# Batch 2's q turned by DMA, and the loads of k gathered behind the copies of v

## The chip, the cores and the metric

One NeuronCore of a Trainium2 chip runs the whole program. The metric is device time in microseconds (us) for one launch. Five engines work side by side, each through its own list in order: PE (matrix products), DVE and ACT (element-wise work), POOL (here also the issuer of all loads from HBM) and SP (here the issuer of DMA transposes and of the stores). They wait for each other by semaphores.

## The reference

Sliding-window attention feeds a two-layer network. For 8 batches, 8 heads, 576 positions and a head size of 64:

```python
scores = (q @ k.transpose(0, 1, 3, 2)) / sqrt(64)
mask = (rel >= 0) & (rel < 64)          # rel = query position - key position
attn = softmax(where(mask, scores, -1e9))
x = (attn @ v).transpose(0, 2, 1, 3).reshape(4608, 512)
h = x @ w_in                            # 512 -> 2048
out = (h * cos(h)) @ w_out              # 2048 -> 512, float32
```

## The kernel before

The 4608 rows of x are cut into 9 tiles of 512 rows, and the network runs tile by tile. Tile 0 and the attention of batches 0 and 1 run in a first part whose order is written out in a long string. After it comes a loop over the tiles 1 to 8; one pass is called a stage here, and stage n is the pass over tile n. In the span of the profiled execution stage 1 starts at 57.4 us, stage 2 at 90.0, stage 3 at 120.5, stage 4 at 150.9, stage 5 at 181.6 and stage 6 at 212.0.

In a stage PE multiplies x by `w_in` (L500, 64 products of 512 columns into `h_ps`); ACT takes the sine (L730) and DVE multiplies it with h (L733); then PE multiplies the result by `w_out` (L744, 64 more products). The last two tiles do this second product by a Strassen-like scheme with 7 products (L587). Between these products PE is given the attention of one batch: stage n scores batch n+1.

The order of that attention work is a plan of due times. A stage has 32 slots; `at(time, fn, ...)` puts a step into the plan, and `pump(time)`, called after every four or so products, emits all steps that are due. What is emitted goes to the end of its engine's list, so a slot sets only the order on each engine; when a step runs is decided by what stands ahead of it and by its semaphores. These steps matter here:

- `load_chunk` (L183) loads 128 rows of q or k of one batch, all heads, cast to bf16, issued on POOL. A batch has 5 chunks, the last one of 64 rows. `load_v` (L189) does the same for v.
- `spread_v` (L127 by the helper `copy`) copies half of v's rows on POOL, so that every window of 128 keys is contiguous.
- `turn_q` and `turn_k` (L244) are DMA transposes issued on SP. Three of them turn the 5 chunks (0 and 1, 2 and 3, 4) of q into `qT` and of k into `kT`. For batch 2, q is instead transposed by PE (`tr_q`, L227, five transposes for each of four head pairs) and copied out of PSUM by DVE (`put_q`, L127).
- `burst_scores` (L331) emits the scores of a batch in two bursts, at slots 14.6 and 20.2. Burst one scores blocks 0 to 3 of the sequence, so it reads chunks 0 and 1 of `qT` and `kT`: the first of the three transposes of each. Burst two reads the others.
- Each group of four score blocks then goes through `g_max` (DVE, L368), `g_exp` (ACT, L380), `g_inv` (DVE, L390), `g_norm` (POOL, L397, which makes `w`) and `g_trans` (a DMA transpose on SP, L416, which makes `wT`). A batch has nine groups; from stage 3 on the first four are normalised before `spread_v` and the last five behind it (stage 1 has three behind it, stage 2 four).
- `values` (PE, L432) multiplies `wT` with v at the end of a stage, and `store` (SP, L509) writes a tile's result in two transfers of 512 KB early in the next stage.

Before the change the chunks of k and q of a batch come alternately, in three pieces: for batches 5 to 7 chunk 0 of both comes two stages ahead, behind the copies of v; chunks 1 and 2 of both and 3 and 4 of q come early in the stage that follows, and chunks 3 and 4 of k behind that stage's copies of v. The three transposes of k are due at slot 26 of that same stage, so on SP they stand ahead of the late `wT` transposes and of the stores.

Of the kernel before, what the change touches and what calls it, by code (L numbers as in the profile page):

```python
# [30 lines left out]
PAIRS = 4  # L31
Q = 16
T = 2 * Q
# [5 lines left out]
BUSY = 8  # L39
NB = 5  # L40
TURNS = ((0, 2), (2, 4), (4, 5))
TURNED = (3, 4, 5, 6, 7)
FAST = (7, 8)
PRODUCTS = ("P1", "P2", "P6", "P5", "P7", "P3", "P4")

# [26 lines left out]
def kernel(  # L72
# [9 lines left out]
    nc = tc.nc  # L82
    B, H, S, D = q.shape
# [17 lines left out]
    qsets = [const.tile([128, NB * PAIRS * 128], BF16, name=f"qT{i}") for i in range(2)]  # L101
# [5 lines left out]
    ident = const.tile([128, 128], BF16, name="ident")  # L107
# [6 lines left out]
    st = {}  # L114
# [11 lines left out]
    def copy(engine, out, in_):  # L126
        {"a": nc.scalar.copy, "p": nc.gpsimd.tensor_copy}.get(engine, nc.vector.tensor_copy)(out, in_)  # L127
# [29 lines left out]
    def head_rows(name, b, p):  # L157
        if (name, b) not in st:
            st[name, b] = rows_tile(name)
        lo = 2 * NC * D * p if b else RC * D + 2 * NC * D * (p - 1)  # L160
        return st[name, b][0:NP, lo:lo + 2 * NC * D].rearrange("p (h x) -> p h x", h=2)
# [48 lines left out]
    def transposed(name, b, p):  # L210
        t_ps = ps_t.tile([128, S], BF16, tag="t", name=f"t{name}_ps")
        of = st[name, b]
        if b == p == 0:
            for c in range(RC):
                for h in range(2):
                    d = slice(64 * h, 64 * h + 64)
                    nc.tensor.transpose(t_ps[d, 64 * c:64 * c + 64], of[d, 64 * c:64 * c + 64], ident[d, d])
        elif b < 2:
            rows = head_rows(name, b, p)
            for c in range(NC):  # L220
                for h in range(2):
                    nc.tensor.transpose(t_ps[64 * h:64 * h + 64, NP * c:NP * c + NP], rows[:, h, D * c:D * c + D],  # L222
                                        ident[:NP, :NP])
        else:
            for c in range(NB):
                n = min(128, S - 128 * c)
                nc.tensor.transpose(t_ps[:, 128 * c:128 * c + n], of[0:n, c, 128 * p:128 * p + 128], ident[0:n, 0:n])  # L227
        return t_ps


    def in_order(t_ps, to, b, p):
        c = RC if b == p == 0 else NC
        return t_ps.rearrange("d (c p) -> d p c", c=c), to.rearrange("d (p c) -> d p c", c=c)

    def by_pair(x):
        return x[:, 0:PAIRS * S].rearrange("d (h s) -> d h s", h=PAIRS)

    def by_chunk(x):
        return x.rearrange("d (c h p) -> d c h p", c=NB, h=PAIRS)
# [12 lines left out]
    def tr_q(b, p):  # L252
        st["tq", b, p] = transposed("q", b, p)

    def put_q(b, p, engine=None):
        if b > 1:
            t_ps, to = st.pop(("tq", b, p)), by_chunk(qsets[b % 2])[:, :, p]
            copy(engine, to[:, 0:4], t_ps[:, 0:512].rearrange("d (c p) -> d c p", c=4))
            copy(engine, to[:, 4, 0:64], t_ps[:, 512:S])
            return  # L260
        of, to = in_order(st.pop(("tq", b, p)), by_pair(qsets[b])[:, p], b, p)
        if b:
            copy(engine, to, of)
        elif engine == "a":
            nc.scalar.mul(to, of, scale)
        else:
            nc.vector.tensor_scalar(to, of, scale, None, ALU.mult)
# [4 lines left out]
    def tr_k(b, p):  # L272
        st["tk", b, p] = transposed("k", b, p)
# [327 lines left out]
    def at(time, fn, *args):  # L601
        plan.append((time, len(plan), fn, args))
# [8 lines left out]
    for i, (b, jobs, banks) in enumerate(bursts):  # L611
        t = T * (b - 1)
        at(t + BURST[i % 2] + 0.9 * (i == 1), burst_scores, i)
        for n in range(jobs[0][0], jobs[-1][-1] + 1):
            place = (n - n_listed) % NU
            time = t + BURST[0] + PACE * place
# [11 lines left out]

    for b in range(2, B):
        t0 = T * (b - 1)  # L630
        for lo, hi in TURNS if b in TURNED else ():
            at(t0 - T + (24.3 if b == 4 else 23.4) + 0.01 * lo, turn_q, b, lo, hi)
        for p in range(0 if b in TURNED else PAIRS):
            t_q = t0 + (2 if b == 2 else 1) + (3.3 if b == 2 else 3.5) * p
            at(t_q, tr_q, b, p)
            at(t_q + 0.02, put_q, b, p)
        if b > 2:
            for c in range(NB):
                for i, name in enumerate(("q", "k")):
                    time = 17.9 + 2.8 * i if b == 3 and c == NB - 1 else 5.6 + 1.6 * c + 0.8 * i  # L640
                    if b > 3 and name == "k" and c > 2:
                        time = (24.2 if b == 4 else 22.4) + 0.01 * c
                    if b > 4 and c == 0:
                        time = (24.26 if b == 5 else 22.46) + 0.01 * i - T
                    at(t0 - T + time, load_chunk, name, b, c)
        for lo, hi in TURNS:
            at(t0 + 0.1 * lo - (2 if b == 2 else 6), turn_k, b, lo, hi)
        for c in range(5):
            at(t0 + (8 if b == B - 1 else 0.5) + c, load_v, b, c)
        for half_ in range(2):  # L650
            if b == 2:
                at(t0 + 24.1 + 0.01 * half_, spread_v, b, half_, "p", 0, 2)
                at(t0 + 24.2 + 0.1 * half_, spread_v, b, half_, "p", 2, 4)
            else:
                at(t0 + (24 if b == 3 else 22.2) + 0.1 * half_, spread_v, b, half_)
    for mt in range(2, n_mt):
        for p in range(PAIRS):
            time = T * mt - (8.01 if mt == n_mt - 1 else 1.01)
# [8 lines left out]
    for n in range(16):  # L667
        i, f = divmod(n, 4)
# [14 lines left out]
    def spread_first(lo, hi):  # L683
# [9 lines left out]
             "io": put_steps, "mk": put_masks, "mc": cast_masks,  # L693
             "tq": lambda p: tr_q(0, p), "tk": lambda p: tr_k(0, p), "Tq": lambda p: tr_q(1, p), "Tk": lambda p: tr_k(1, p),
             "pq": lambda p, engine: put_q(0, p, engine), "pk": lambda p, engine: put_k(0, p, engine),
             "Pq": lambda p, engine: put_q(1, p, engine), "Pk": lambda p, engine: put_k(1, p, engine),
             "zA": spread_first(0, 1), "zB": spread_first(1, 3), "zC": lambda engine: spread_v(0, 1, engine, 3, 4),
             "yA": lambda engine: spread_v(1, 0, engine, 0, 2), "yB": lambda engine: spread_v(1, 0, engine, 2, 3),
# [85 lines left out]
```

## Time and profile before

| what | value |
|---|---|
| three runs, median | 301.48 us (301.41 to 301.97) |
| profiled execution, own time | 301.49 us |
| its span (first to last instruction) | 299.7 us |
| PE busy | 291.8 us, 97% of the span |
| DVE, ACT, POOL busy | 230.9, 232.3, 205.2 us |
| PE's share of the chain that ended last | 89% |

The profiled execution's own time is 1.8 us above its span. Rows of the timeline and of the chain give a start and a duration in us, then engine, line, operation, what is written and read, and how many instructions are merged. A row marked SPq or POOL with DMA in its name is the issue of a transfer, not the transfer; the time from issue to landing stands in a row of its own. "Idle before" and "<-" give how long the engine stood idle ahead of the row and what released it.

### The profile page before, as it was taken

What the parts mean: (1) busy time and instruction counts of PE and PEld (TensorE: products, weight loads), DVE (VectorE), ACT (ScalarE), POOL (GpSimd) and SP (SyncE); (2) the same over time, 40 slices, a digit from 0 to 9 for tenths busy, and PEclk for the clock granted to TensorE, in tenths of its full rate; (3) what the DMA queues carried; (4) which work ended last, traced back from release to release, by engine and by line L of the source; (5) the groups of instructions that cost most, each with busy time, mean ns of one, the idle gap of its engine ahead of it and who ended that gap; (6) DMA issues with size and microseconds to landing.
All of it is one profiled execution on the core that took longest, in us unless ns stands there. A gap on an engine that the chain in (4) does not pass through costs nothing.

```text
span 299.7 us, 8184 instructions
## 1 busy us (share of the span) xinstructions
PE 291.8 (97%) x2787; PEld 159.7 (53%) x2787; DVE 230.9 (77%) x904; ACT 232.3 (77%) x781; POOL 205.2 (68%) x226
## 2 busy tenths in 40 slices
PE   8978999999999999999999999999999999999995
PEld 3667854544454444444454545444544454784584
DVE  4998788988887786788677866887588658976793
ACT  5997699876988799869986998699969996305600
POOL 9898668993699849995999599949997850000000
PEclk9999999999999999999999999999999999999999
DMA  7999999999999995999999999999999443003013
GB/s 147 175 204 191 196 190 141 113 138 148 234 165 121 202 175 99 167 143 229 152 171 139 178 164 199 142 230 165 152 121 189 70 88 142 0 3 140 3 35 107
DMA packets 165867, 43.22 MB, mean 144 GB/s; under 512 B 153216, under 2 KB 161472, under 8 KB 165824
## 3 DMA queue, kind: packets, MB, share of 16 engines
q0 software_dynamic: 100896, 18.06, 81.6%
q1 hardware_dynamic: 64784, 24.56, 45.7%
q8 instruction: 22, 0.36, 0.5%
q14 instruction: 21, 0.17, 0.2%
q10 hardware_dynamic: 144, 0.07, 0.1%
HBM read 36.70 MB, written 9.44 MB: 154 GB/s over the span
## 4 chain that ended last, share of the span: by engine, by line
PE 89%; DMA 6%; POOL 2%; DVE 0%; issue 0%; POOLq 0%
PE h_ps L500 37%; PE out_ps L744 28%; PE out_ps L587 8%; PE out_ps L483 5%; DMA w_in<-in_moe_w_in_dram 4%; PE h_ps L464 4%; PE o_ps L432 3%; PE s_ps L331 3%; DMA q<-in_q_dram 2%; POOL v L189 1%; PE s_ps L353 1%; PE tq_ps L227 0%; POOL w_in L205 0%; PE tw_ps L413 0%; POOL q L166 0%
## 5 line engine op out<-in xcount | busy, mean ns | idle before, releaser
L500 PE MATMUL h_ps<-xT,w_in 128*128 128x512 bf16 x512 | 112.5, 379 | 0.2
L733 DVE TENSOR_TENSOR gT<-h_ps,sin 128x512 bf16<-128x512 f32 x128 | 84.9, 688 | 27.3 <-ACT sin L730 27.3
L730 ACT ACTIVATE sin<-h_ps 128x512 f32<-128x512 f32 x128 | 73.8, 598 | 34.8 <-PE h_ps L500 32.6
L380 ACT ACTIVATE e<-s,negm 128x128 f32<-128x128 f32 (+1 forms) x256 | 97.2, 382 | 1.7 <-POOL v L127 0.9
L397 POOL TENSOR_TENSOR w<-e,rden 128x512 bf16<-128x512 f32 (+1 forms) x68 | 69.0, 1029 | 28.8 <-DVE rden L390 21.1
L744 PE MATMUL out_ps<-w_out,gT 128*128 128x512 bf16 x384 | 85.3, 379 | 0.0
L500 PEld LDWEIGHTS <-w_in 128*128 128x128 bf16 x512 | 49.7, 98 | 58.3
L744 PEld LDWEIGHTS <-gT 128*128 128x128 bf16 x384 | 36.5, 98 | 43.1
L368 DVE CUSTOM_DVE_ANT_0 s<-s_ps,mask 128x128 f32<-128x128 f32 (+1 forms) x256 | 56.0, 276 | 1.8 <-PE s_ps L353 1.5
L380 ACT ACTIVATION_READ_ACCUMULATOR e<-s,negm 128x1 f32 x256 | 48.3, 189 | 0.0
L189 POOL DMA_DIRECT2D v<-in_v_dram x40 | 34.1, 877 | 0.6 <-DMA q<-in_q_dram 0.6
L183 POOL DMA_DIRECT2D q<-in_q_dram x30 | 26.4, 883 | 4.6 <-PE tq_ps L222 2.6
L183 POOL DMA_DIRECT2D k<-in_k_dram x30 | 26.3, 886 | 0.6 <-DMA v<-in_v_dram 0.6
L390 DVE RECIPROCAL rden<-den 128x4 f32<-128x4 f32 (+1 forms) x73 | 12.2, 167 | 18.4 <-ACT e L380 18.1
L127 POOL COPY v<-v 64x1536 bf16<-64x1536 bf16 (+3 forms) x16 | 22.9, 1431 | 0.4
L368 DVE DVE_READ_ACCUMULATOR2_ANT negm<- 128x1 f32 x256 | 21.0, 82 | 0.1
L127 DVE CAST xT<-o_ps 128x512 bf16<-128x512 f32 x24 | 15.5, 677 | 4.7 <-PE o_ps L432 4.5
L464 PE MATMUL h_ps<-xT,w_in 128*128 128x256 bf16 x128 | 14.6, 273 | 0.9 <-DMA w_in<-in_moe_w_in_dram 0.9
L483 PE MATMUL out_ps<-w_out,gT 128*128 128x512 bf16 x64 | 14.8, 380 | 0.0
L464 PEld LDWEIGHTS <-w_in 128*128 128x128 bf16 x128 | 12.3, 98 | 2.3 <-DMA w_in<-in_moe_w_in_dram 1.0
L587 PEld LDWEIGHTS <-sums 128*128 128x128 bf16 x136 | 12.2, 98 | 2.0 <-DVE sums L532 0.4
L470 ACT ACTIVATE sin<-h_ps 128x512 f32<-128x512 f32 x16 | 9.2, 596 | 4.3 <-PE h_ps L464 4.3
(92 smaller groups left out, 293.0 us busy)
## 6 DMA issues: line engine op xcount, KB each, us to landing
out_dram<-out_sb SPq DMA_DIRECT2D x16, 512.0 KB, 8.0
v<-in_v_dram POOLq DMA_DIRECT2D x32, 128.0 KB, 6.2
q<-in_q_dram POOLq DMA_DIRECT2D x24, 128.0 KB, 9.5
k<-in_k_dram POOLq DMA_DIRECT2D x24, 128.0 KB, 9.4
w_in<-in_moe_w_in_dram POOLq DMA_DIRECT2D x4, 512.0 KB, 8.7
w_out<-in_moe_w_out_dram POOLq DMA_DIRECT2D x4, 512.0 KB, 10.9
q<-in_q_dram POOLq DMA_DIRECT2D x7, 144.0 KB, 6.2
k<-in_k_dram POOLq DMA_DIRECT2D x7, 144.0 KB, 6.3
```

What stands on the lines that cost most here:

```text
L127: {"a": nc.scalar.copy, "p": nc.gpsimd.tensor_copy}.get(engine, nc.vector.tensor_copy)(out, in_)
L183: nc.gpsimd.dma_start(out=st[name, b][0:n, c].rearrange("p (h d) -> p h d", h=H), in_=src.rearrange("h p d -> p h d"))
L189: nc.gpsimd.dma_start(out=vt.rearrange("p (h d) -> p h d", h=H), in_=v[b, :, c * 128:c * 128 + n, :].rearrange("h p d -> p h d"))
L368: nc.vector.tensor_tensor_reduce(out=s[:, u, c], in0=s_ps[:, u, c], in1=mask[:, 2 - j % 2 if j else 0, c], scale=-scale if b else -1.0, sc ...
L380: nc.scalar.activation(e[:, u, c], s[:, u, c], AF.Exp, bias=negm[:, u:u + 1], scale=1.0 if n < n_first else -1.0, accum_out=den[:, u:u + 1])
L397: (nc.gpsimd if engine == "p" else nc.vector).tensor_tensor(out=w[:, 0:u], in0=e[:, 0:u], op=ALU.mult, in1=rden[:, 0:u].unsqueeze(2).to_br ...
L464: nc.tensor.matmul(out=h_ps[:, half * e:half * e + half], lhsT=w_in_sb[:, ks, ff * 128:ff * 128 + 128], rhs=st["xT", 0][:, ks, half * g:ha ...
L500: nc.tensor.matmul(out=st["h", ff], lhsT=w_in_sb[:, ks, ff * 128:ff * 128 + 128], rhs=st["xT", mt][:, ks], start=start, stop=stop)
L587: nc.tensor.matmul(out=to[n_] if split else to[:, e], lhsT=lhs[name][f // 2][:, f % 2, 128 * e:128 * e + 128], rhs=rhs[name][:, f, lo:hi], ...
L730: nc.scalar.activation(sin, h_ps, AF.Sin, bias=math.pi / 2.0)
L733: nc.vector.tensor_tensor(out=gt[:, e], in0=h_ps, in1=sin, op=ALU.mult)
L744: nc.tensor.matmul(out=o_ps[e], lhsT=gT[ff // 2][:, ff % 2, ms * 128:ms * 128 + 128], rhs=w_out_sb[:, ff], start=ff == 0, stop=ff == n_ff - 1)
```

## The change

Three things are done, all in the plan:

1. q of batch 2 is turned by three DMA transposes like the later batches, alternating on SP with the three of k. The 20 PE transposes and 8 DVE copies for it go, and so does the code for them.
2. All five chunks of k of batches 3 to 7 are loaded in one stretch, behind the copies of v of the stage before the one that scores them (due at slot 24.3, from batch 5 on 22.5). Their three transposes move from slot 26 of that stage to slots 1.6, 3.6 and 5.6 of the next, the stage that scores them.
3. The five chunks of q of batches 3 to 7 are loaded in one stretch, at slots 4.9 to 8.1; v's loads come 0.8 slots apart from batch 3 on, and those of batch 7 at slot 0.5 in place of 8.

The core of the diff:

```diff
-        for lo, hi in TURNS if b in TURNED else ():
-            at(t0 - T + (24.3 if b == 4 else 23.4) + 0.01 * lo, turn_q, b, lo, hi)
-        for p in range(0 if b in TURNED else PAIRS):
-            t_q = t0 + (2 if b == 2 else 1) + (3.3 if b == 2 else 3.5) * p
-            at(t_q, tr_q, b, p)
-            at(t_q + 0.02, put_q, b, p)
-        if b > 2:
-            for c in range(NB):
-                for i, name in enumerate(("q", "k")):
-                    time = 17.9 + 2.8 * i if b == 3 and c == NB - 1 else 5.6 + 1.6 * c + 0.8 * i
...
-                    at(t0 - T + time, load_chunk, name, b, c)
         for lo, hi in TURNS:
-            at(t0 + 0.1 * lo - (2 if b == 2 else 6), turn_k, b, lo, hi)
-        for c in range(5):
-            at(t0 + (8 if b == B - 1 else 0.5) + c, load_v, b, c)
+            at(t0 - (2.01 - 0.1 * lo if b == 2 else T - (24.3 if b == 4 else 23.4) - 0.01 * lo), turn_q, b, lo, hi)
+        for lo, hi in TURNS:
+            at(t0 + (0.1 * lo - 2 if b == 2 else 1.6 + lo), turn_k, b, lo, hi)
+        for c in range(NB):
+            if b > 2:
+                at(t0 - T + 4.9 + 0.8 * c, load_chunk, "q", b, c)
+                at(t0 - (7.7 if b < 5 else 9.5) + 0.01 * c, load_chunk, "k", b, c)
+            at(t0 + 0.5 + (1 if b == 2 else 0.8) * c, load_v, b, c)
```

POOL's list from the first norms of stage 3 (batch 4) to the loads early in stage 4; `v_77` is the buffer of v of batch 4, `v_78` that of batch 5, and the k loaded here is that of batch 5 (before: chunks 3 and 4 of batch 5, then chunk 0 of q and k of batch 6). Before:

```order
L397 TENSOR_TENSOR w<-e,rden 128x512 x4
L127 COPY v_77<-v_77 64x3x512
L127 COPY v_77<-v_77 64x4x512
L183 DMA k<-in_k_dram 128x8x64
L183 DMA k<-in_k_dram 64x8x64
L183 DMA q<-in_q_dram 128x8x64
L183 DMA k<-in_k_dram 128x8x64
L397 TENSOR_TENSOR w<-e,rden 128x512 x5
L189 DMA v_78<-in_v_dram 128x8x64 x4
L189 DMA v_78<-in_v_dram 64x8x64
```

After:

```order
L387 TENSOR_TENSOR w<-e,rden 128x512 x4
L126 COPY v_77<-v_77 64x3x512
L126 COPY v_77<-v_77 64x4x512
L182 DMA k<-in_k_dram 128x8x64 x4
L182 DMA k<-in_k_dram 64x8x64
L387 TENSOR_TENSOR w<-e,rden 128x512 x5
L188 DMA v_78<-in_v_dram 128x8x64 x4
L188 DMA v_78<-in_v_dram 64x8x64
L182 DMA q<-in_q_dram 128x8x64 x4
L182 DMA q<-in_q_dram 64x8x64
```

Five loads stand between the copies and the last five norms in place of four, and the loads of k early in the stage are gone.

SP's list from the first `wT` of stage 3 to the first `wT` of stage 4; `qT_76` and the `kT` here belong to batch 5, which stage 4 scores. Before:

```order
L416 DMA_TRANSPOSE wT<-w 128x4x128 x4
L244 DMA_TRANSPOSE qT_76<-q 128x8x128 x2
L244 DMA_TRANSPOSE qT_76<-q 128x4x64
L416 DMA_TRANSPOSE wT<-w 128x4x128 x2
L244 DMA_TRANSPOSE kT<-k 128x8x128 x2
L244 DMA_TRANSPOSE kT<-k 128x4x64
L416 DMA_TRANSPOSE wT<-w 128x4x128 x3
L509 DMA out_dram<-out_sb 128x2x512 x2
```

After:

```order
L406 DMA_TRANSPOSE wT<-w 128x4x128 x4
L239 DMA_TRANSPOSE qT_76<-q 128x8x128 x2
L239 DMA_TRANSPOSE qT_76<-q 128x4x64
L406 DMA_TRANSPOSE wT<-w 128x4x128 x5
L499 DMA out_dram<-out_sb 128x2x512 x2
L239 DMA_TRANSPOSE kT<-k 128x8x128 x2
L239 DMA_TRANSPOSE kT<-k 128x4x64
```

The three transposes of k have moved from between the late `wT` to behind all five of them and behind both stores.

SP's list in stage 1, from the three of k of batch 2 on. Before:

```order
L244 DMA_TRANSPOSE kT<-k 128x8x128 x2
L244 DMA_TRANSPOSE kT<-k 128x4x64
L416 DMA_TRANSPOSE wT<-w 128x4x128 x2
L509 DMA out_dram<-out_sb 128x2x512 x2
L416 DMA_TRANSPOSE wT<-w 128x4x128 x4
```

After:

```order
L239 DMA_TRANSPOSE qT_75<-q 128x8x128
L239 DMA_TRANSPOSE kT<-k 128x8x128
L239 DMA_TRANSPOSE qT_75<-q 128x8x128
L239 DMA_TRANSPOSE kT<-k 128x8x128
L239 DMA_TRANSPOSE qT_75<-q 128x4x64
L239 DMA_TRANSPOSE kT<-k 128x4x64
L406 DMA_TRANSPOSE wT<-w 128x4x128 x2
L499 DMA out_dram<-out_sb 128x2x512 x2
```

The second transpose of k has one more ahead of it, the third two more. On PE, nothing changes but that the 20 transposes and their weight loads are gone.

More of the change, by code (lines that the diff above doesn't have):

```diff
@@ L41 @@
 TURNS = ((0, 2), (2, 4), (4, 5))
-TURNED = (3, 4, 5, 6, 7)
 FAST = (7, 8)
@@ L217, in transposed @@
                     nc.tensor.transpose(t_ps[d, 64 * c:64 * c + 64], of[d, 64 * c:64 * c + 64], ident[d, d])
-        elif b < 2:
+        else:
             rows = head_rows(name, b, p)
@@ L223, in transposed @@
                                         ident[:NP, :NP])
-        else:
-            for c in range(NB):
-                n = min(128, S - 128 * c)
-                nc.tensor.transpose(t_ps[:, 128 * c:128 * c + n], of[0:n, c, 128 * p:128 * p + 128], ident[0:n, 0:n])
         return t_ps
@@ L255, in put_q @@
     def put_q(b, p, engine=None):
[L256 to L260, printed above, removed]
         of, to = in_order(st.pop(("tq", b, p)), by_pair(qsets[b])[:, p], b, p)
@@ L630 @@
         t0 = T * (b - 1)
-        for lo, hi in TURNS if b in TURNED else ():
-            at(t0 - T + (24.3 if b == 4 else 23.4) + 0.01 * lo, turn_q, b, lo, hi)
-        for p in range(0 if b in TURNED else PAIRS):
-            t_q = t0 + (2 if b == 2 else 1) + (3.3 if b == 2 else 3.5) * p
-            at(t_q, tr_q, b, p)
-            at(t_q + 0.02, put_q, b, p)
-        if b > 2:
-            for c in range(NB):
-                for i, name in enumerate(("q", "k")):
-                    time = 17.9 + 2.8 * i if b == 3 and c == NB - 1 else 5.6 + 1.6 * c + 0.8 * i
[L641 to L644, printed above, removed]
-                    at(t0 - T + time, load_chunk, name, b, c)
-        for lo, hi in TURNS:
-            at(t0 + 0.1 * lo - (2 if b == 2 else 6), turn_k, b, lo, hi)
-        for c in range(5):
-            at(t0 + (8 if b == B - 1 else 0.5) + c, load_v, b, c)
+        for lo, hi in TURNS:
+            at(t0 - (2.01 - 0.1 * lo if b == 2 else T - (24.3 if b == 4 else 23.4) - 0.01 * lo), turn_q, b, lo, hi)
[6 more added lines that the diff above has]
+            at(t0 + 0.5 + (1 if b == 2 else 0.8) * c, load_v, b, c)
         for half_ in range(2):
```

## The prediction

> **What bounds the kernel now.** I read the chain that ended last first. The rows below are from it: the four groups of PE transposes of q of batch 2 (L227), and the first burst of scores of stages 1 to 6 (L331). A row is start, duration, what. Behind it stands one row of the windows view: length of stage 3, then busy time of PE, PEld, DVE, ACT and POOL, the granted clock, the DMA share and GB/s.
>
> ```profile
> 59.98 0.35 PE tq_ps L227 x5
> 63.90 0.36 PE tq_ps L227 x5
> 66.95 0.35 PE tq_ps L227 x5
> 70.00 0.36 PE tq_ps L227 x5
> 73.05 0.52 PE s_ps L331 x32
> ...
> 103.97 0.52 PE s_ps L331 x32
> ...
> 134.44 0.52 PE s_ps L331 x32
> ...
> 164.91 0.52 PE s_ps L331 x32
> ...
> 195.55 0.52 PE s_ps L331 x32
> ...
> 226.02 0.52 PE s_ps L331 x32
> ```
>
> ```profile
> 120.44:150.90 30.46, 30.43 (x264) 14.58 (x265) 23.03 (x108) 27.07 (x95) 26.70 (x29) 1.00 1.78 177
> ```
>
> PE is busy for 30.43 of a stage's 30.46 us, at full clock, and the first bursts follow each other by 30.5 to 30.9 us. So from stage 1 on PE alone sets the pace: what leaves its list there is gained whole, and any wait that is put into it is paid whole. Nothing else has to be sped up; it must only not come late. The question is whether the data of each first burst are still early.
>
> The second view is the timeline of POOL at the end of stage 3, with the same place (norm, copies of v) of other stages. It shows when the loads of k can be issued.
>
> ```profile
> 83.96 4.22 POOL L127 COPY v<-v 64x1024 bf16<-64x1024 bf16 x4
> ...
> 114.88 3.41 POOL L127 COPY v<-v 64x1536 bf16<-64x1536 bf16 x2
> ...
> 143.80 3.41 POOL L127 COPY v<-v 64x1536 bf16<-64x1536 bf16 x2
> ...
> 150.60 5.03 POOL L397 TENSOR_TENSOR w<-e,rden 128x512 bf16<-128x512 f32 x5
> 155.59 4.25 POOL L189 DMA_DIRECT2D v<-in_v_dram  x5
> ...
> 174.34 3.40 POOL L127 COPY v<-v 64x1536 bf16<-64x1536 bf16 x2
> ...
> 204.97 3.40 POOL L127 COPY v<-v 64x1536 bf16<-64x1536 bf16 x2
> ```
>
> The copies of stage 3 end at 147.2, the last five norms start at 150.60, behind four loads, and run back to back: POOL has no slack there. The third view is SP's timeline at the same place, in which `kT` is issued 10.7 us ahead of its burst at 164.91.
>
> ```profile
> 151.66 2.50 SPq L416 DMA_TRANSPOSE wT<-w  x2
> 154.26 4.40 SPq L244 DMA_TRANSPOSE kT<-k  x3
> 158.75 4.53 SPq L416 DMA_TRANSPOSE wT<-w  x3
> 163.39 1.12 SPq L509 DMA_DIRECT2D out_dram<-out_sb  x2
> ```
>
> **The change part by part.** *The PE transposes of q.* Four groups, 0.35 + 0.36 + 0.35 + 0.36 = 1.42 us, all in the chain, with products of PE on both sides: −1.42 us. The DVE copies that go with them lay beside PE's work: nothing.
>
> *The DMA transposes of q that come instead.* The first one stands ahead of the first of k on SP and needs chunks that were loaded long before. The first of k, which burst one waits for, keeps its place behind the load of its chunks. This is its issue and its time to landing in stage 1:
>
> ```profile
> L244 SPq DMA_TRANSPOSE kT<-k x1: 1247/1247/1247, 61.4 to 61.4; - x1
> DMA to landing us min/median/max: 6.8/6.8/6.8
> ```
>
> It lands at 68.2; the burst will be due at 73.05 − 1.42 = 71.6. The cover is 3.4 us. The later ones slip by one or two issues, and burst two stands 5.6 slots behind burst one, about 5 us at 30.46 us for 32 slots; three loads of k fewer compete with them there. I cost this at nothing; without the cover, each us that the transpose is late would be a us.
>
> *The loads of k and their transposes.* This part decides. Every time below is on the clock of before; the 1.42 us shift both sides alike. Take the transposes for stage 4's burst. POOL: copies end at 147.2; five loads take 4.25 us (the row of five loads of v), where four took 3.4; the first of the five norms ends 1.0 us later (5.03 for five), at 152.5. SP then issues five `wT`, 1.3 us each (its three-transpose rows come to 1.3 to 1.5 each; it is slower than POOL's 1.0, so it sets the pace), until 159.0, the two stores (1.12, with their waits 1.2) until 160.2, and only then the first transpose of k. That is copies' end + 6.5 + 1.3 for each `wT`: 13.0 us for five norms, 11.7 for four (stage 2), 10.4 for three (stage 1). Slot 1.6 is about 152.4 in PE's time, but SP gets there 8 us later. Queued behind these transposes are only the next `wT`, which come later anyway.
>
> Issued at 160.2 against a burst at 164.91, it has 4.7 us to land. What landings cost, in rows: the first transpose of k in stages 6 and 4, with nothing but `wT` ahead; the second of stage 4, issued 1.4 us later, when the loads of v had begun; the stores of stage 6, with the loads of v issued one at a time; the stores of stage 4, with v and then q and k loading in one row.
>
> ```profile
> L244 SPq DMA_TRANSPOSE kT<-k x1: 1265/1265/1265, 214.2 to 214.2; - x1
> DMA to landing us min/median/max: 3.2/3.2/3.2
> ...
> L244 SPq DMA_TRANSPOSE kT<-k x1: 1267/1267/1267, 154.3 to 154.3; - x1
> DMA to landing us min/median/max: 3.7/3.7/3.7
> ...
> L244 SPq DMA_TRANSPOSE kT<-k x1: 1267/1267/1267, 155.6 to 155.6; - x1
> DMA to landing us min/median/max: 6.3/6.3/6.3
> ...
> L509 SPq DMA_DIRECT2D out_dram<-out_sb x2: 375/442/509, 223.3 to 224.2; - x2
> DMA to landing us min/median/max: 5.0/5.2/5.4
> ...
> L509 SPq DMA_DIRECT2D out_dram<-out_sb x2: 482/507/532, 163.4 to 164.0; - x2
> DMA to landing us min/median/max: 9.3/9.8/10.4
> ```
>
> What SP issues lands in the order of issue: 158.0, 161.9, then the stores at 172.7 and 174.4. So the transpose of k lands behind 1 MB of stores that were issued 1.2 and 0.6 us ahead of it. Low end: the second store takes 5.4 as in stage 6, that is 4.8 after our issue, and our transpose 1.3 more (the time of one transpose by its issue row): 6.1 us. High end: the store takes 10.4 as in stage 4, 9.8 after our issue, and the transpose 3.9 more (158.0 to 161.9, beside the loads of v): 13.7. Below the low end nothing is left, since no row has a store that passes an earlier transfer. In the new order v's five loads are issued at 156.5, 2.5 us ahead of the stores, and q's five follow, so the loads compete as in stage 4; but fewer transposes stand ahead of the stores (two that are still moving, where there were four). I take 9.3, near the middle. In the last loop, into stage 6, only v follows, no q, and I take 6.9.
>
> [...]
>
> A wait also gives something back. These two rows of ACT follow the burst at 134.44:
>
> ```profile
> 135.09 1.28 ACT L492 ACT_TABLE_LOAD   x1
> ...
> 136.50 0.33 ACT L380 ACTIVATE e<-s,negm 128x64 f32<-128x64 f32 x1
> ```
>
> The first exponential starts 2.06 us after the burst because the last sine and the table load are in its way. When PE has waited, both are done, and the first exponential needs only the score matmuls and one DVE step, about 0.75 us. So norms, copies, loads and the next transpose all come 1.3 us earlier, in each stage whose own burst has waited (all but stage 1).
>
> The sum, burst by burst: copies' end, plus SP's way, plus landing, less the burst's time, less 1.3.
> Stage 2: 88.2 + 10.4 + 9.3 = 107.9, against 103.97: 3.9.
> Stage 3: 118.3 + 11.7 + 9.3 = 139.3, against 134.44, less 1.3: 3.6.
> Stage 4: 147.2 + 13.0 + 9.3 = 169.5, against 164.91, less 1.3: 3.3.
> Stage 5: 177.7 + 13.0 + 9.3 = 200.0, against 195.55, less 1.3: 3.2.
> Stage 6: 208.4 + 13.0 + 6.9 = 228.3, against 226.02, less 1.3: 1.0.
> Together 15.0 us of waits. Each counts whole, since the next burst's transpose is again counted from the burst before it, not from PE's free time.
>
> *The rest.* q's loads come earlier and together, and are turned as before at slot 23.4 or so, 15 slots later. v of batch 7 moves ahead of POOL's eight sums of weights (L520), which are read only in stage 7; the norms behind them in stage 6 may start a little later, but the `values` at that stage's end need only one of them. The late norms of every stage slip by the fifth load, 0.85 us, and their `wT` are needed only at the end of the next stage. Nothing, all three.
>
> Total: 301.49 − 1.42 + 15.0 = 315.1 on the profiled execution's own time, which is the runs' median within 0.01; I forecast 315.0.
>
> **The rivals.** *A, faster: the transposes land in time.* If the first transpose of k takes 3.7 us or a little more from its issue, as at 154.3, it lands at 164, ahead of the burst, and only the gain is left: 301.49 − 1.42 = 300.1. It decides at 4.7 us in stages 3 to 5 and 5.4 in stage 2. For it speaks that stores alone may be fast; against it that 1 MB of stores is ahead in the same queue and that landings keep the order of issue. [...]
>
> *B, no change: waits that just eat the gain.* At the low end of 6.1 (4.5 in the last loop) the waits are 0.7, 0.4, 0.1, 0 and 0, together 1.2: 301.3.
>
> *C, slower still: the waits let PE's clock drop.* PE would stand for 3.2 to 3.9 us before four of the bursts, where before it is idle for 0.03 us in a whole stage, so the 1.00 above says nothing of that. If it comes back at half clock, each of the four long waits ends in a burst of 1.04 us in place of 0.52, and the slack behind takes up the rest: + 2.1, so 317.1. [...]
>
> That the change doesn't do what it says is excluded by the new lists of PE, POOL and SP.
>
> **How the numbers follow.** Forecast 0.69, A 0.11, B 0.05, C 0.15. Under the forecast alone, with landings between the two ends, the time lies between 303 and 323; the high end itself, 13.7 everywhere, would give waits of about 35 us and 335, which would need the worst row in every stage. The range goes down to B and leaves out A and what lies above 323: 301.0 to 323.0. About 0.2% is what a measurement of this kernel can tell from no change, 0.6 us. Faster: A, 0.11. Within: B, 0.05. Slower: the forecast and C, 0.84.
>
> **What would show it right or wrong.** Right: the 20 transposes are gone and stage 1 is 1.4 us shorter; in stages 2 to 6 the chain of waits has a DMA of `kT` just ahead of L321, 1 to 5 us long, and PE is idle there; the first transpose of k is issued behind the stores, 10 to 13 us after the copies of v; the first exponential comes under 1 us after the burst. Wrong: `kT` lands ahead of its burst in all stages (then A), or PE waits at another place: burst two, or `values` for a late `wT`. A granted clock under 1.00 in the windows of stages 2 to 6 would be C.

## The result, and the profile after

The changed kernel takes 338.30 us (median of 4 runs, 337.42 to 340.03), beside 301.45 us for the kernel before. The ratio is 1.1226 [1.1179, 1.1273]. The profiled execution of it took 338.54 us, with a span of 336.8. In some runs of this study the chip itself was disturbed; ratios leave such runs out, while medians are over all runs, so that the two do not always agree (least of all for both edits together, where two of four runs are left out and the median is 308.85 us).

The chain that ended last, of the kernel after: start, duration, what. These are the first burst of scores of the stages 1 to 6 (L321 now), and what it waited for.

```profile
70.37 0.52 PE s_ps L321 x32
...
95.91 11.24 DMA kT<-k
...
107.19 0.96 PE s_ps L321 x19
...
134.96 12.00 DMA kT<-k
...
147.09 0.96 PE s_ps L321 x26
...
174.09 11.30 DMA kT<-k
...
185.53 0.96 PE s_ps L321 x25
...
213.24 10.57 DMA kT<-k
...
223.94 0.96 PE s_ps L321 x25
...
251.41 9.12 DMA kT<-k
...
260.67 0.96 PE s_ps L321 x26
...
269.09 0.80 PE s_ps L321 x40
```

Before, the chain at these places was PE alone. Now a transpose of k stands ahead of every burst from stage 2 on, and each follows the one before it by 36.7 to 39.9 us in place of 30.5 to 30.9. The burst takes 0.96 us in place of 0.52 (the timeline, which lets a full-speed burst start 0.07 us earlier, has 0.59): PE comes back at half clock. In the windows view the granted clock is 0.50 from 143.11 to 149.94, about the burst at 147.09. One row of the waits view and one of the windows view (columns as in the prediction, from the burst of stage 3 to that of stage 4) say the same of the whole and of one loop.

```profile
PE s_ps L321 <- DMA kT<-k: 28.4, 5, 6.9
```

```profile
147.09:185.53 38.44, 31.52 (x261) 15.11 (x266) 23.20 (x107) 27.45 (x94) 26.22 (x27) 0.94 1.55 135
```

PE is idle for 6.9 of 38.4 us, and the mean granted clock is 0.94. The waits come to 28.4 us; the kernel lost 37.

In the same loop, POOL and SP:

```profile
157.00 3.41 POOL L126 COPY v<-v 64x1536 bf16<-64x1536 bf16 x2
160.36 4.27 POOL L182 DMA_DIRECT2D k<-in_k_dram  x5
164.69 5.03 POOL L387 TENSOR_TENSOR w<-e,rden 128x512 bf16<-128x512 f32 x5
```

```profile
158.93 4.35 SPq L239 DMA_TRANSPOSE qT<-q  x3
165.75 7.01 SPq L406 DMA_TRANSPOSE wT<-w  x5
172.87 1.12 SPq L499 DMA_DIRECT2D out_dram<-out_sb  x2
174.09 8.35 SPq L239 DMA_TRANSPOSE kT<-k  x3
```

The copies end at 160.4, and the first transpose of k is issued 13.7 us later, behind five `wT` and both stores. The tiles view has the two stores, and the transpose by itself:

```profile
L499 SPq DMA_DIRECT2D out_dram<-out_sb x2: 494/508/521, 172.9 to 173.5; - x2
...
DMA to landing us min/median/max: 6.5/7.3/8.0
...
L239 SPq DMA_TRANSPOSE kT<-k x1: 3307/3307/3307, 174.1 to 174.1; - x1
...
DMA to landing us min/median/max: 11.3/11.3/11.3
```

The second store lands at 173.5 + 8.0 = 181.5, and the transpose at 185.4, 3.9 us behind it. Last, ACT and DVE after the burst at 147.09, from the timeline; the bracket has the idle time ahead of the row and what ended it.

```profile
147.99 0.35 ACT L370 ACTIVATE e<-s,negm 128x64 f32<-128x64 f32 x1 [5.63 <-DVE negm L358]
...
154.08 0.40 ACT L370 ACTIVATE e<-s,negm 128x128 f32<-128x128 f32 x1 [1.58 <-DVE negm L358]
```

```profile
152.60 0.69 DVE L126 COPY out_sb<-out_ps 128x512 f32<-128x512 f32 x1 [1.99 <-PE out_ps L724]
```

The first exponential comes 0.90 us after the burst, as forecast (2.06 before). But 6 us later ACT stands idle for 1.58 us, because DVE, which works in order, waits for PE's product into `out_ps`, and PE, at half clock until 149.94, comes to it late.

From the chain, POOL's copies and the landings, the five loops as they were forecast and as they came (us; a loop runs from one first burst to the next):

| loop, into stage | burst to copies' end, forecast / measured | to the issue of kT | to its landing | loop, forecast / measured |
|---|---|---|---|---|
| 2 | 15.1 / 16.0 | 10.4 / 9.5 | 9.3 / 11.2 | 34.8 / 36.8 |
| 3 | 13.0 / 16.0 | 11.7 / 11.8 | 9.3 / 12.0 | 34.0 / 39.9 |
| 4 | 11.5 / 13.3 | 13.0 / 13.7 | 9.3 / 11.3 | 33.8 / 38.4 |
| 5 | 11.5 / 14.6 | 13.0 / 13.1 | 9.3 / 10.6 | 33.8 / 38.4 |
| 6 | 11.5 / 14.2 | 13.0 / 13.3 | 6.9 / 9.1 | 31.4 / 36.7 |
| sum | 62.7 / 74.1 | 61.1 / 61.4 | 44.1 / 54.2 | 167.9 / 190.3 |

The measured loops have 0.6 us more in all between landing and burst. The forecast was 15.0 us above the loops of before, the measurement 37.3. With the gain of stage 1 (burst at 70.37 in place of 73.05, −2.7) and the stretch from the last first burst to the end of the span (336.8 − 260.67 = 76.1 against 299.7 − 226.02 = 73.7, +2.4) this gives 37.0; the profiled executions differ by 338.54 − 301.49 = 37.05.

### The profile page after: what moved, and what is told of

Same layout as the page of the kernel before. It is cut to its first block, busy times and chain, and to the rows that moved or that the text cites. A ratio compares the mean times of both kernels' runs of the same rounds, so it can differ in the third digit from the quotient of the medians.

```text
span 336.8 us, 8113 instructions
## 1 busy us (share of the span) xinstructions
PE 298.9 (89%) x2736; PEld 162.7 (48%) x2767; DVE 229.9 (68%) x896; ACT 234.0 (69%) x781; POOL 204.9 (61%) x226
## 4 chain that ended last, share of the span: by engine, by line
PE 74%; DMA 17%; ACT 3%; DVE 2%; issue 2%; POOL 1%; SPq 0%; POOLq 0%
PE out_ps L724 27%; PE h_ps L490 22%; DMA kT<-k 16%; PE out_ps L577 7%; PE h_ps L454 4%; PE out_ps L473 4%; PE s_ps L321 3%; PE o_ps L422 2%; ACT e L370 2%; PE busy L133 1%; PE s_ps L343 1%; ACT sin L710 1%; PE tw_ps L403 1%; POOL v L188 1%; DMA v<-in_v_dram 1%
## 5 line engine op out<-in xcount | busy, mean ns | idle before, releaser
L370 ACT ACTIVATE e<-s,negm 128x128 f32<-128x128 f32 (+1 forms) x256 | 97.3, 383 | 35.9 <-DVE negm L358 35.8
L490 PE MATMUL h_ps<-xT,w_in 128*128 128x512 bf16 x497 | 111.0, 379 | 1.0
L710 ACT ACTIVATE sin<-h_ps 128x512 f32<-128x512 f32 x128 | 73.7, 599 | 34.9 <-PE h_ps L490 34.2
L724 PE MATMUL out_ps<-w_out,gT 128*128 128x512 bf16 x372 | 92.1, 406 | 1.9 <-issue 1.8
L490 PEld LDWEIGHTS <-w_in 128*128 128x128 bf16 x512 | 50.0, 98 | 59.2
L724 PEld LDWEIGHTS <-gT 128*128 128x128 bf16 x384 | 38.9, 104 | 50.3 <-issue 13.1
L321 PE MATMUL s_ps<-kT,qT 64*64 64x128 bf16 (+1 forms) x432 | 10.8, 245 | 28.5 <-DMA kT<-k 28.4
L182 POOL DMA_DIRECT2D q<-in_q_dram x30 | 25.4, 891 | 4.5 <-issue 2.4
L182 POOL DMA_DIRECT2D k<-in_k_dram x30 | 25.5, 872 | 0.0
L321 PEld LDWEIGHTS <-qT 64*64 64x64 bf16 x432 | 8.4, 126 | 33.9 <-issue 27.9
L380 DVE RECIPROCAL rden<-den 128x4 f32<-128x4 f32 (+1 forms) x73 | 12.2, 167 | 14.0 <-ACT e L370 13.7
L126 DVE COPY out_sb<-out_ps 128x512 f32<-128x512 f32 x16 | 11.0, 689 | 14.4 <-PE out_ps L724 14.3
L454 PE MATMUL h_ps<-xT,w_in 128*128 128x256 bf16 x128 | 14.6, 273 | 0.0
L473 PE MATMUL out_ps<-w_out,gT 128*128 128x512 bf16 x60 | 14.3, 379 | 0.3 <-issue 0.2
## 6 DMA issues: line engine op xcount, KB each, us to landing
w_out<-in_moe_w_out_dram POOLq DMA_DIRECT2D x4, 512.0 KB, 10.6
```

What stands on the lines that cost most here:

```text
L182: nc.gpsimd.dma_start(out=st[name, b][0:n, c].rearrange("p (h d) -> p h d", h=H), in_=src.rearrange("h p d -> p h d"))
L321: nc.tensor.matmul(out=to.rearrange("p (a t) -> p a t", a=chunks), lhsT=blocks_of(qsets[b % 2], b, pe, j, 1)[d, 0], rhs=rhs[d], start=True ...
L370: nc.scalar.activation(e[:, u, c], s[:, u, c], AF.Exp, bias=negm[:, u:u + 1], scale=1.0 if n < n_first else -1.0, accum_out=den[:, u:u + 1])
L454: nc.tensor.matmul(out=h_ps[:, half * e:half * e + half], lhsT=w_in_sb[:, ks, ff * 128:ff * 128 + 128], rhs=st["xT", 0][:, ks, half * g:ha ...
L490: nc.tensor.matmul(out=st["h", ff], lhsT=w_in_sb[:, ks, ff * 128:ff * 128 + 128], rhs=st["xT", mt][:, ks], start=start, stop=stop)
L710: nc.scalar.activation(sin, h_ps, AF.Sin, bias=math.pi / 2.0)
```

## The experiments

Theory: a transpose of k that is issued behind `wT` and stores lands late, and PE waits. Rivals: the loads of k, not the turns, are what costs; the clock alone makes the loss; q of batch 2 is not free. Eight of the ten ran beside runs of the kernel before with a median of 301.16 us; the second run of the turns at their old place and the one with both edits beside 301.77.

**q of batch 2 by DMA, and nothing else.**

```diff
-TURNED = (3, 4, 5, 6, 7)
+TURNED = (2, 3, 4, 5, 6, 7)
-            at(t0 - T + (24.3 if b == 4 else 23.4) + 0.01 * lo, turn_q, b, lo, hi)
+            at(t0 - 2.01 + 0.1 * lo if b == 2 else t0 - T + (24.3 if b == 4 else 23.4) + 0.01 * lo, turn_q, b, lo, hi)
```

> The kernel before, with q of batch 2 turned by DMA and nothing else of the change. Theory (the loss comes from the turns of k standing behind the late wT and the stores on SP): the 20 transposes leave PE's list, burst one of stage 1 finds its data, no burst waits: 1.4 us under the kernel before, 300.1. Rival (the three extra DMA transposes of stage 1 hold up stage 1 or 2): PE waits at a burst of stage 1, 302 or more.

Measured: 303.58 us (12 runs), ratio 1.0047 [1.0013, 1.0081]: slower, a miss. The waits view has a wait that before has not, and the tiles view the two `wT` that it is about, in this run and in before:

```profile
PE o_ps L432 <- DMA wT<-w: 3.2, 3, 1.8
```

```profile
L416 SPq DMA_TRANSPOSE wT<-w x2: 1232/1778/2323, 81.0 to 82.4; - x2
...
DMA to landing us min/median/max: 7.4/7.8/8.1
```

```profile
L416 SPq DMA_TRANSPOSE wT<-w x2: 1189/1203/1217, 81.1 to 82.7; - x2
...
DMA to landing us min/median/max: 3.7/4.4/5.1
```

The `values` at the end of stage 1 wait 1.83 us for a `wT` that lands at 90.5 and not at 86.4. (Another 1.19 of the 3.2 us lie at 56.5, ahead of the loads of batch 3; the next run, with the same transposes, has no wait there.) Behind the wait PE is slow: from 92.47 on six products by `w_in` take 2.56 us in the chain, 0.43 each, where 46 of them took 9.93, 0.22 each, from 58.49 on. So it is 34.8 us from burst one of stage 1 to that of stage 2, in place of 30.9. Three more transposes stand on the DMA engines beside eight loads of q and k of batch 3, and the two `wT` behind them land 2.2 and 4.1 us later. So the gain of 1.42 us on PE is not to be had by this edit alone.

**The same, with the loads of k of batch 3 behind the copies of v.**

```diff
+                    if b == 3 and name == "k":
+                        time = T - 7.7 + 0.01 * c
                     at(t0 - T + time, load_chunk, name, b, c)
```

> The kernel before with q of batch 2 turned by DMA and, other than in the run with that alone (303.58 us), the five loads of k of batch 3 moved behind stage 1's copies of v. Theory (turning q of batch 2 by DMA loses only because eight loads of q and k in a row stand ahead of the transposes and wT of stage 1 on the DMA engines): the wait for wT at the end of stage 1 goes, 300.1 us, range 299.4 to 301.0, ratio 0.996. Rival (three more transposes in stage 1 cost that by themselves): 302.5 to 304.5.

Measured: 300.67 us (12 runs), ratio 0.9984 [0.9961, 1.0006], inside the theory's range and outside the rival's. The waits for `wT` fall from 3.2 to 1.3 us, 0.6 the longest, and none of them is in stage 1. So it takes both: the transposes of q cost something only beside all of these loads, and the loads without the transposes do no harm in the kernel before. The gain that is left, 0.16%, is not clear of noise.

**The change with the turns of k where they were before.**

```diff
-            at(t0 + (0.1 * lo - 2 if b == 2 else 1.6 + lo), turn_k, b, lo, hi)
+            at(t0 + 0.1 * lo - (2 if b == 2 else 6), turn_k, b, lo, hi)
```

> The changed kernel with only the slots of the turns of k put back to where they were (slot 26 of the stage before); the loads of k and q stay as changed. Theory: on SP the turns stand ahead of the last three wT and of the stores again, kT is there some 5 us ahead of every burst, no waits: 300.1, clock 1.00 throughout. Rival (the five loads of k in one stretch, in front of the late norms on POOL, are what costs): most of the loss stays, over 320.

Measured: 300.05 us (12 runs), ratio 0.9975 [0.9942, 1.0007], near the theory's 300.1 and far from the rival's 320; a gain over the kernel before is not yet clear of noise. All of the loss is gone, with k still loaded late. The first transpose for the burst of stage 4, and the burst:

```profile
L239 SPq DMA_TRANSPOSE kT<-k x1: 2514/2514/2514, 154.1 to 154.1; - x1
...
DMA to landing us min/median/max: 6.5/6.5/6.5
```

```profile
163.62 0.59 PE L321 MATMUL s_ps<-kT,qT 64*64 64x64 bf16 x32
```

It lands at 160.6, 3 us ahead. The late loads cost something (before, it landed 3.7 us after its issue), but the cover holds it.

**The same once more**, for a narrower interval.

> The best version so far once more, with k turned at the place where the kernel before has it and everything else as changed, to narrow its interval: theory (20 transposes of 71 ns less on PE, and no wait of PE for k): ratio 0.995 to 0.999 to the kernel before, about 300.2 us. Rival (no difference): ratio 0.9995 to 1.002.

Measured: 300.67 us (12 runs), ratio 0.9955 [0.9934, 0.9977]. This version beats both kernels, by 0.45%.

**The change with the stores behind the transposes of k.**

```diff
-                at(base + T + 0.5 + ms0 / 2, store, o_sb, mt, ms0, 0, 2)
+                at(base + T + 8 + ms0 / 2, store, o_sb, mt, ms0, 0, 2)
```

> The changed kernel with the stores of tiles 1 to 6 at slots 8 and 9 in place of 0.5 and 1, so that on SP the turns of k stand ahead of them, still behind all late wT. Theory: the first turn of k is issued 1.2 us earlier and has no 1 MB of stores ahead: it lands 5 to 6.5 us after its issue (as 6.3 before) in place of 11, 6 us earlier in each stage; waits of 0 to 2 us remain: 302 to 309. Rival (the stores matter only by their 1.2 us of issue, the loads of v and q set the landing): landing stays at 10 to 11 us, 330 to 334.

Measured: 305.16 us (4 runs), ratio 1.0146 [1.0083, 1.0209].

```profile
PE s_ps L321 <- DMA kT<-k: 4.2, 4, 1.5
```

```profile
152.20 6.44 SPq L406 DMA_TRANSPOSE wT<-w  x5
158.75 6.15 SPq L239 DMA_TRANSPOSE kT<-k  x3
165.00 1.03 SPq L499 DMA_DIRECT2D out_dram<-out_sb  x2
```

The first transpose is issued 11.9 us after the copies' end (146.9) and lands 7.5 us later. Without the stores ahead it saves 1.2 us of issue and some 4 of landing. The waits are short, 1.5 at most, the clock stays at 0.999 and the copies come earlier: of 37 us only some 4.4 are left. The stores ahead of the transposes are the largest single part of the loss.

**The change, with PE kept busy ahead of each burst one from batch 3 on** (20 products whose results nobody reads).

```diff
         b, jobs, banks = bursts[n]
+        if b > 2 and n % 2 == 0:
+            keep_busy(20)
```

> The changed kernel with 20 products of 512 columns more ahead of burst one of batches 3 to 7 (work that is thrown away), 4.3 us of PE time inside waits of 5.5 to 6.9 us. If the clock's drop after the wait costs time of its own (bursts of 0.96 in place of 0.52 us, products at half speed behind it): granted clock 1.00 throughout, burst one to burst two 5.8 us in place of 7.2 to 8.4, each loop some 1.3 us shorter, 2.6 in the last stage: 330 to 331. If the half clock only fills time that is waited anyway: 336 to 338. If the extra products are not hidden: over 340.

Measured: 329.71 us (4 runs), ratio 1.0946 [1.0888, 1.1004]; so the half clock costs some (1.1226 − 1.0946) x 301.3 = 8.4 us, and that is rather too little, since one of the five bursts still took 0.91 us (at 182.66) and in the last loop the added products end 1.6 us behind the landing. Stage 3's burst, with the last of the added products ahead of it:

```profile
142.67 1.67 PE L133 MATMUL busy<-w_out 128*128 128x512 bf16 x7
145.09 0.59 PE L323 MATMUL s_ps<-kT,qT 64*64 64x64 bf16 x32 [0.74 <-DMA kT<-k]
```

The copies of v behind it start at 153.69, 8.6 us after the burst; in the changed kernel it was 157.00 − 147.09 = 9.9. The loops are still 35 to 39 us long: in the first four, whatever PE does meanwhile, k's chain (copies, SP's list, landing) sets them. So the clock is a part, and not the whole.

**The change with the loads of k behind the late norms.**

```diff
-                at(t0 - (7.7 if b < 5 else 9.5) + 0.01 * c, load_chunk, "k", b, c)
+                at(t0 - 0.5 + 0.01 * c, load_chunk, "k", b, c)
```

> Theory (the first transpose of k is issued late because its stage's five late norms stand on POOL behind five loads of k, 4.3 us in stage 3 of the changed kernel, and the wT and both stores behind the norms): with the loads behind the norms instead, norms, wT and stores come some 4.3 us earlier in each of the stages 2 to 6, the transpose is issued at the end of the copies of v + 9 in place of + 13, and each wait of PE shrinks by about that: 338.3 - 5 x 4.3 = 317, range 312 to 323, the lower end if the TensorE clock comes back up with the waits. Rival (the transposes are held by the loads alone, which now come later still): no gain or a loss, 335 to 345.

Measured: 327.33 us (4 runs), ratio 1.0851 [1.0802, 1.0901]. That is between the two; neither had it right.

```profile
153.44 3.41 POOL L126 COPY v<-v 64x1536 bf16<-64x1536 bf16 x2
156.93 4.03 POOL L387 TENSOR_TENSOR w<-e,rden 128x512 bf16<-128x512 f32 x4
```

```profile
155.37 3.96 SPq L239 DMA_TRANSPOSE qT<-q  x3
159.42 7.45 SPq L406 DMA_TRANSPOSE wT<-w  x5
166.98 1.12 SPq L499 DMA_DIRECT2D out_dram<-out_sb  x2
169.37 7.78 SPq L239 DMA_TRANSPOSE kT<-k  x3
```

The norms do start at once behind the copies, 4.3 us earlier. But SP's own list, three transposes of q and five `wT` back to back, is nearly as long, and the first `kT` comes 12.5 us after the copies' end (156.85) in place of 13.7. For the last 1.2 us of that SP is done with the stores and waits for rows of k, whose loads are issued from 163.11 on now. Over the five loops the issue gains 2.8 us in all. The landing, 9.3 to 10.1 us in place of 9.1 to 12.0, gains 6.1 over the five; what in the new order makes it shorter was not taken apart.

**Both of these edits.**

> Both of two earlier edits: the stores of the stages' results behind the transposes of k, and the loads of k behind the late norms. Theory (the late norms are not what holds the transposes, since SP's own list from the transposes of q to the fifth wT is about as long as POOL's; with the loads behind the norms the rows of k themselves land only some 12.5 us after the copies of v, as in the run with that edit alone, and that becomes what the transpose waits for): the transpose is issued about 12 us after the copies in place of 10.6 with the stores' edit alone, so it is later, not earlier, 305.2 + 5 x 1.4 = 312, range 307 to 317. Rival (five loads ahead of the norms on POOL are what is left of the delay): the remaining 4.2 us of waits go, 300.3 to 302.

Measured: ratio 1.0154 [1.0109, 1.0200] (4 runs), beside 1.0146 for the stores alone. The rival falls; the theory's size does too.

```profile
150.96 7.52 SPq L406 DMA_TRANSPOSE wT<-w  x5
160.86 5.95 SPq L239 DMA_TRANSPOSE kT<-k  x3
```

SP is done with the `wT` at 158.5 and waits 2.4 us for rows of k: issue at copies' end (148.4) + 12.5, as expected. It then lands in 6.9, so that PE waits 5.3 us in all, near the 4.2 of the stores' edit.

**The change with the first output block's copy later in DVE's list.**

```diff
-                            copy("a" if e and (mt > 1 or ms0) else "d", o_sb[:, e], o_ps[e])
+                            if e or ms0 or mt == n_mt - 1:
+                                copy("a" if e and (mt > 1 or ms0) else "d", o_sb[:, e], o_ps[e])
+                            else:
+                                at(base + 21.5, copy, "d", o_sb[:, e], o_ps[e])
```

> Theory (part of what I took as given back is not: behind a late burst DVE's list has the copy of the first output block, which waits for PE at half clock, ahead of the row maxima of the burst's fourth group, so that ACT idles some 1.6 us and the last norms, the wT and the next transposes of k come that much later in each loop): with that copy behind two more groups' maxima each of the loops of the stages 2 to 6 is 1.0 to 1.7 us shorter, 338.3 - 5 x 1.4 = 331, range 329 to 334. Rival (the norms' time is set elsewhere, by the exponentials or the copies of v): 337 to 339.

Measured: 339.09 us (4 runs), ratio 1.1220 [1.1160, 1.1281]: nothing, a miss. DVE and POOL after the burst at 146.11 of this run:

```profile
154.24 0.29 DVE L358 CUSTOM_DVE_ANT_0 s<-s_ps,mask 128x128 f32<-128x128 f32 x1 [2.52 <-PE s_ps L321]
```

```profile
155.94 1.04 POOL L387 TENSOR_TENSOR w<-e,rden 128x512 bf16<-128x512 f32 x1 [3.10 <-DVE rden L380]
```

The wait for the copy is gone, and DVE waits 2.52 us one place further on, for the scores of burst two, which PE, with 0.96 us for its burst and 6.86 us for the 24 products behind it, reaches just as late (at 153.79). The fourth norm ends no earlier. It is PE's slow stretch behind the burst, not this copy, that takes the norms' lead away; the run with PE kept busy is the one that gives it back.

**The change without q's loads of batches 4 to 7.**

```diff
     def load_chunk(name, b, c):
+        if name == "q" and b > 3:
+            st["q", b] = st["q", 3]
+            return
```

> Leaves out the loads of q of the batches 4 to 7 (their transposes read batch 3's rows again). Theory (a transpose of k takes 10 to 12 us from issue to landing in the stages 2 to 5 because the loads of v and q fill the DMA engines beside it; in stage 6, where no q is loaded, it took 9.1): landing 9 to 10 us in the stages 2 to 5, and 338.3 - 4 x 2 = 330, range 325 to 334. Rival (it waits for the stores ahead of it in SP's queue, or is slow by itself): 337 to 339.

Measured: 333.94 us (4 runs), ratio 1.1086 [1.1035, 1.1138], at the upper edge of the theory's range.

```profile
L242 SPq DMA_TRANSPOSE kT<-k x1: 2997/2997/2997, 171.2 to 171.2; - x1
...
DMA to landing us min/median/max: 9.2/9.2/9.2
```

Into stage 4 the landing was 11.3 in the changed kernel, and is 9.2 (into stage 3 12.0 and 9.6). Over the stages 2 to 5 q's loads beside it are worth 0.8 to 2.4 us of the landing, and the stores ahead about 4 (7.5 without them).

## Why the prediction was wrong in size

The direction and the place were right: PE waits for the first transpose of k in the stages 2 to 6, behind `wT` and stores. The time fell far outside the range (338.3 against 301 to 323), because two terms of the sum were mis-sized.

- *q of batch 2: right.* Burst one of stage 1 is 2.7 us earlier and does not wait, though its transpose landed 6.2 us after its issue at 60.7. Beyond the 1.42 it is mostly a wait of 0.9 us for `w_in` ahead of it, which before's profile has and this one has not. The clause that fewer loads of k compete there did more than I gave it: without it the edit loses.
- *The issue of the first transpose: right.* 61.1 us over the five loops, 61.4 measured. My reason was partly wrong: the five loads ahead of the norms on POOL are not the whole cause that I made them, since SP's list is nearly as long by itself: without them it still ends 11.3 us behind the copies (at 168.1 in the run with the loads behind the norms).
- *"I take 9.3, near the middle": the first failed step.* 44.1 us were forecast, 54.2 came, +10.1. I took the mean of an end in which both the store and the transpose are fast, and one in which both are slow. The stores came near the middle (8.0 between 5.4 and 10.4), but the transpose behind them took 3.9, the slow value: 7.4 + 3.9 = 11.3. A transpose beside running loads had its own row, 157.9 to 161.9, and the loads were there for certain.
- *"All come 1.3 us earlier": the second failed step.* 62.7 us were forecast from the bursts to the copies' end, 74.1 came, +11.4. The first exponential is early, as I said. But its groups are fed from PE through DVE's list, and after these waits PE ran at half clock (0.50). Behind the bursts at 107.19, 147.09, 185.53 and 223.94 it does so for 5.2, 2.9, 5.4 and 4.5 us, and the copies end 2.5, 1.3, 2.6 and 2.1 us later than where the clock held behind such a burst (in the runs with the stores behind and with PE kept busy, 13.6 us in loop 3 and 12.1 in the later ones): about half of each stretch, 8.5 of the 11.4. Another 0.9 lies in loop 2, which starts from a burst that had not waited; these two runs have the same there within 0.1 us. The rest is the lead: where PE came back at full clock it was real but smaller. With the stores behind, the copies end 12.1 us after the waiting bursts at 166.27 and 197.62, against 12.8 before, 0.8 of my 1.3. Where the other 0.5 is was not looked into.
- *Rival C, the clock: right in kind, 2.1 us in price, 8.4 measured.* The half stood on no row of before; the waits of the changed kernel show it, 0.50 in the windows view. I priced the four bursts at it and left the rest to slack. There is none: PE's products are slow for up to 5.4 us behind a burst, and the chain to the next transpose of k hangs on them. The profile with PE kept busy has 6.7 us less between the bursts and the copies' ends (67.4 against 74.1) and 2.6 less at the end of the program (73.5 against 76.1); SP's list takes 2.9 back on the way to the issue (64.3 against 61.4). That profile is only 6.5 us shorter in all, being of the slowest of its four runs, 332.07 us.

The windows view of the changed kernel has five stretches of 6.83 us at half clock, one with each wait (columns as in the prediction):

```profile
105.57:112.40 6.83, 5.00 (x42) 2.30 (x44) 2.66 (x27) 4.32 (x23) 1.03 (x1) 0.50 1.61 125
143.11:149.94 6.83, 2.85 (x37) 1.49 (x38) 2.04 (x22) 1.95 (x11) 0.12 (x1) 0.50 2.23 145
184.07:190.90 6.83, 5.15 (x42) 2.40 (x44) 2.80 (x27) 4.48 (x24) 1.03 (x1) 0.50 1.46 117
221.62:228.45 6.83, 4.29 (x40) 2.10 (x42) 2.71 (x27) 3.61 (x20) 1.03 (x1) 0.50 1.72 135
259.17:266.00 6.83, 5.11 (x42) 2.40 (x44) 2.71 (x27) 4.44 (x24) 2.44 (x3) 0.50 0.38 62
```

They begin inside the waits, 1.5 to 4.0 us ahead of the bursts. The length of a wait does not decide alone. In the timeline waits of 0.8 to 1.5 us (the run with the stores behind) all end in a burst of 0.59 us, as where there is no wait, and waits of 4.05 to 6.9 us (the changed kernel) all in one of 0.96. Between them 2.53 us (both edits), 3.36 and 3.38 us end in 0.96, but 3.56 us in 0.59 (all three with the loads behind the norms, where 4.03 us end in 0.66). The shortest of these that ended in 0.96, from the run with both edits, and two of the run with the loads behind the norms:

```profile
134.94 0.96 PE L321 MATMUL s_ps<-kT,qT 64*64 64x64 bf16 x32 [2.53 <-DMA kT<-k]
```

```profile
215.63 0.96 PE L321 MATMUL s_ps<-kT,qT 64*64 64x64 bf16 x32 [3.36 <-DMA kT<-k]
...
251.31 0.59 PE L321 MATMUL s_ps<-kT,qT 64*64 64x64 bf16 x32 [3.56 <-DMA kT<-k]
```

What decides between these was not shown.

The terms are not independent: a late transpose slows PE, that makes the norms late, and that the next transpose. With this it fits that the stores, out of the way, save 6.5 us of issue and 18.4 us of landing over the five loops (54.9 and 35.8 us are left), but (1.1226 − 1.0146) x 301.3 = 32.5 as measured: the copies' ends, with the clock at 0.999, come another 7.7 us earlier (66.4 in place of 74.1). What stays open is how the DMA engines share between v's, k's and q's loads, the stores and the transposes: the runs price two of these, not the rule.

## What to carry to other kernels

A load may be moved late (300.05 us with the loads of k late and their transposes early), but a transpose that PE waits for is kept ahead of the stores in its queue (305.16 us against 338.30), and its landing is priced from a row with the same loads beside it, not from the middle between a best and a worst row. Where waits like these are put into a loop that PE bounds, what follows is priced at half clock too, in-order lists that PE feeds included: here each of the five waits of 4.05 to 6.9 us came with 6.83 us at a granted clock of 0.50. An edit that moves work from PE to the DMA engines is tried together with what makes room there: alone it lost 0.5%; with the loads of k moved away it measured 0.2 to 0.5% faster in three series of runs, of which only the last, 0.45%, is clear of noise.

## What the runs showed of the hardware

- A DMA transpose of 128 rows by 1024 columns landed 3.2 us after its issue with only `wT` ahead of it and the last load beside it landing 0.3 us after that issue (the kernel before, stage 6), 6.4 to 7.5 beside loads (the run with the stores behind), 9.1 to 10.4 with 1 MB of stores ahead of it and loads of v beside (the run without q's loads), and 10.6 to 12.0 with q's loads too (the changed kernel, stages 2 to 5).
- With 20 products in the wait four of five bursts came at 0.59 us; one, behind a remaining wait of 2.0 us, still took 0.91.
- In the changed kernel the granted clock was 0.50 for 6.83 us with each of the five waits of 4.05 to 6.9 us. A wait of 2.53 us (both edits) ended in a burst of 0.96 us, waits of 0.8 to 1.5 us (the run with the stores behind) in bursts of 0.59. Behind a wait of 1.83 us (q of batch 2 alone, with one of 0.18 us just ahead of it) six products took 0.43 us each in place of 0.22.
- SP took a transpose every 1.3 us (6.44 us for five `wT`, the run with the stores behind); three transposes of q and five `wT` in a row took it 11.5 us (155.37 to 166.87 in the run with the loads behind the norms).
